# Layer two's second products: tokens or weights as the stationary side, and another table of priorities

## The chip, the cores and the metric

The kernel runs on one core of one Trainium2 chip. Times are device microseconds of one execution. An execution that is profiled also has a span, which the profiler counts from the core's first instruction to its last; the device time lies a little above it. The engines are PE (TensorE matmuls), PEld (TensorE weight loads), DVE (VectorE), ACT (ScalarE), POOL and SP, which issues nearly all transfers.

## The reference

Local attention over 3072 tokens (24 tiles of 128), then two layers of the same shape, each a product into 2048 hidden columns, a gate, and a product back to 512:

```python
x = attention(q, k, v, mem_k, mem_v)                 # 3072 x 512
h = x @ moe_w_in                                     # 512 -> 2048
x = (s * np.maximum(h, 0.0) ** 2 + b) @ moe_w_out    # 2048 -> 512
h = x @ moe2_w_in
g = h * (1.0 / (1.0 + np.exp(-1.702 * h)))
return (g @ moe2_w_out).astype(np.float32)           # 3072 x 512
```

All inputs are float32 (the weights come in a wider form, of which the kernel makes float32 words).

## The kernel before

Every product that needs float32 accuracy is made of three matmuls in the faster fp32r form: each operand is cut into a high part (a cast) and a low part (what the cast left over), and high by high, high by low and low by high are added up in PSUM.

The work on PE has three parts. First come attention for all tiles, woven together with layer one for 2048 of the tokens (lines 711 and 744, `step`). Then four stages of `wino(s)` follow, each for 1024 tokens in two blocks `bp` and `bq` of 512. `SEVEN` lists them: stage 0 is the rest of layer one (`m = 0`), stages 1 to 3 are layer two (`m = 1`). A stage does both of its large products with seven block products in place of eight, after Winograd.

In a stage, the first products (`product`, lines 1082 to 1084) make the gated hidden values G, in eight chunks `p` of 128 hidden rows by 512 tokens for each of four types. The second products then run seven times, in the order `n = 0, 4, 1, 5, 3, 6, 2`, each over eight chunks `p`; one call of `outer_product(n, p, ...)` is one chunk of one product. It takes G's high and low part (`gh`, `gl`, 128 by 512 tokens) and the weights' high and low part (`wh`, `wl`, 128 by 256 output columns), and adds to a pair of PSUM banks.

The two layers differed in how this was done. For `m = 0` the weights are stationary in two pieces of 128 output columns and 512 tokens stream past (line 1243): six matmuls of 512 columns, output with columns on the partitions. For `m = 1` the tokens are stationary in four pieces of 128 and 256 weight columns stream past (line 1237): twelve matmuls of 256 columns, output with tokens on the partitions, as the result wants it:

```python
if m:
    for t in range(4) if only is None else only:
        ...
        for x, (lt, rh) in enumerate(((gh, wh), (gh, wl), (gl, wh))):
            nc.tensor.matmul(a, lt[:, z], rh, ...)
```

What feeds these chunks is `split` (lines 1204 and 1207): ACT casts two chunks of G at once into a tile `kh`, and DVE subtracts to make `kl`. There are three pairs of such tiles (two in the ring `wj`, one in the ring `q`; the trace calls them `oj` and `oq`). ACT's cast for a pair therefore waits until PE has read the last of that pair. Weights come by SP (line 1182) into a ring of eight. For the products 3, 6 and 2, DVE first adds or subtracts types of G (line 1216). After the seven products DVE and ACT add the banks up in a tile `ys` (lines 1253, 1265, 1306), and SP stores (lines 1272, 1274). The very last product of the last stage is cut into pieces (`only`), with its own additions and stores in `last` (lines 1290 and 1295).

The order of all work is fixed when the program is built. `Plan.order` lists every operation with a due time, moves the due times by the table `SHIFTS` (operation number, how many from there on, by how much), and then picks for each engine what is due first among what is ready in its own model of times. Where the model sees PE idle at the start, it puts in filler matmuls (line 1407, `idle`).

Of the kernel before, what the change touches and what calls it, by code (L numbers as in the profile page):

```python
# [12 lines left out]
ALU = mybir.AluOpType  # L13
AX = mybir.AxisListType

P = 128
# [4 lines left out]
NT = B * S  # L21
DM = H * D
DFF = 2048
KT = DM // P
# [77 lines left out]
)  # L102
# [174 lines left out]
def attention_moe_moe(ctx: ExitStack, tc: tile.TileContext, q_t, k_w, v_w, w_in1, w_out1, s_b, w_in2, w_out2, out):  # L277
# [504 lines left out]
    def finish(m, b, k, group, lo, hi, after, need):  # L782
# [16 lines left out]
        def store(e):  # L799
            if m == 0:  # L800
                dst = y1[k, :, b * 512:b * 512 + 512]
            else:
                dst = out[(4 * b + k) * P:(4 * b + k + 1) * P, :]
            nc.sync.dma_start(out=dst, in_=T["y", m, b, k])

# [222 lines left out]
    def wino(s):  # L1028
# [189 lines left out]

        extra = ("turn", s, "a", 2)

        def outer_product(n, p, need, key, d, after, only=None):
            tag, turn = BANKS[n]
            held = ("turn", s, tag, turn)
            ending = s == len(SEVEN) - 1 and n == 2
            first = n != 5 and p == 0

            def fn(e):
                acc = psum(tag, held)
                gh, gl = [T[key + (v,)][:, p % 2] for v in "hl"]
                wh, wl = [w[:, p % 2 * 256:p % 2 * 256 + 256] for w in T["wp", s, n, p // 2]]  # L1230
                if m:
                    for t in range(4) if only is None else only:
                        z = slice(t * P, t * P + P)
                        own = ending and t == 3
                        a = psum("a", extra)[:, 0][:, :256] if own else acc[:, t // 2, t % 2 * 256:t % 2 * 256 + 256]
                        for x, (lt, rh) in enumerate(((gh, wh), (gh, wl), (gl, wh))):
                            nc.tensor.matmul(a, lt[:, z], rh, start=first and (own or t % 2 == 0) and x == 0,  # L1237
                                             stop=p == HALF - 1 and x == 2, skip_group_check=True)
                else:
                    for k in range(2):  # L1240
                        z = slice(k * P, k * P + P)
                        for x, (lt, rh) in enumerate(((wh, gh), (wh, gl), (wl, gh))):
                            nc.tensor.matmul(acc[:, k], lt[:, z], rh, start=first and x == 0,  # L1243
                                             stop=p == HALF - 1 and x == 2, skip_group_check=True)
            return op(need, {"pe": 0.36 * len(only) if only is not None else 1.44 if m else 1.36}, fn, after=o_part[n, p // 2] + [d] + after, alloc=taken(tag, held) + (taken("a", extra) if ending else []),
                      uses=[("wp", s, n, p // 2), key + ("h",), key + ("l",), held] + ([extra] if ending else []))

# [10 lines left out]
        def away(n, b, in1, need, after, lo, q, where=None):  # L1258
# [8 lines left out]
            def store(e):  # L1267
                t = (bq if q else bp) * 512
                if m:
                    r = t + b * 256  # L1270
                    dst = out[r:r + 256, 0 if lo else 256:256 if lo else 512].rearrange("(t p) d -> p t d", p=P)
                    nc.sync.dma_start(out=dst, in_=T[key].rearrange("p (t d) -> p t d", t=2))
                else:
                    nc.sync.dma_start(out=y1[(0 if lo else 2) + b, :, t:t + 512], in_=T[key])
            d = op(need, {"dve": 0.69}, fn, after=(o_end[n] if held else []) + after, alloc=[("y", key)] if where is None else [],
# [8 lines left out]
        def last(n, b, part, need, after, end):  # L1284
            held = ("turn", s) + BANKS[n]
            lo, hi = (part, part + 1) if b else (0, 2)
            z = slice(256 * lo, 256 * hi)

            def fn(e):
                nc.vector.tensor_tensor(out=spot(b)[:, z], in0=T[extra][:, 0][:, :256] if b and part else T[held][:, b][:, z], in1=spot(b)[:, z], op=ALU.add)  # L1290

            def store(e):
                r = bp * 512 + b * 256
                dst = out[r + lo * P:r + hi * P, 256:512].rearrange("(t p) d -> p t d", p=P)
                nc.sync.dma_start(out=dst, in_=spot(b)[:, z].rearrange("p (t d) -> p t d", t=hi - lo))
            d = op(need, {"dve": 0.42 if b else 0.69}, fn, after=[end] + after, uses=[tmp, extra if b and part else held])
            o = op(need, {"sp": 0.37 if b else 0.73}, store, after=[d], uses=[tmp])
            plan.soon.update((d, o))
# [12 lines left out]
        for i, n in enumerate((0, 4, 1, 5, 3, 6, 2)):  # L1311
# [3 lines left out]
            for x in range(HALF // 2):  # L1315
# [8 lines left out]
                for p in (2 * x, 2 * x + 1):  # L1324
                    if s == len(SEVEN) - 1 and n == 2 and p == HALF - 1:
                        prev = [outer_product(n, p, here + 8 * p + only[0], key, d, prev + wait, only) for only in ((0, 1), (2,), (3,))]
                    else:
                        prev = [outer_product(n, p, here + 8 * p, key, d, prev + wait)]
            o_end[n] = prev
            e = here + 66  # L1330
            for b in range(2):
# [9 lines left out]
                elif n == 6:  # L1341
                    got["u4", b] = evac(n, b, b, b, e, [got["u2", b], got["c21", b]])
                    got["c22", b] = away(None, b, b, e, [got["u4", b], got["y7", b]], False, True, 2 + b)
                elif n == 2:
                    if s == len(SEVEN) - 1:
                        for part in range(b + 1):
                            last(n, b, part, e, [got["u4", b], got["c22", b]], o_end[n][b + part])
                    else:
                        away(n, b, b, e, [got["u4", b], got["c22", b]], False, False, b)
# [61 lines left out]

_OUTS = [((NT, DM), "float32")]

# [52 lines left out]
```

## Time and profile before

| | us |
|---|---|
| median of 3 runs | 1062.87 (1062.79 to 1063.54) |
| profiled execution, device time | 1063.68 |
| its span | 1061.9 |
| PE busy | 1049.8 (99%) |
| DVE busy | 758.4 (71%) |
| ACT busy | 602.4 (57%) |
| transfers | 265.67 MB, 250 GB/s over the span |

The profiled execution took 0.81 us longer than the median of the runs. A row of the page's fifth part reads: line, engine, operation, what is written from what, shape, count, then busy time and mean duration of one. Matmuls are pipelined, so the duration of one matmul record is longer than its pace; the pace is read from the starts of matmuls that follow each other, or from the length of a long run of them in the chain of work.

### The profile page before, as it was taken

Reading aid. Unit: us, or ns where it says so; the run is one execution under the profiler, and the core shown is the slowest. Engines: PE = TensorE matmul, PEld = TensorE weight load, DVE = VectorE, ACT = ScalarE, POOL = GpSimd, SP = SyncE. Lnnn points to the kernel's source line nnn. Section 1 sums busy time; section 2 is a strip of 40 time slices with the busy share of each in tenths; the row PEclk is TensorE's granted clock in tenths of the full one; section 3 lists DMA queues with packets and bytes.
Section 4 is the critical chain, followed back from the end, with each engine's and each line's share of the span. In section 5 each row is a group of like instructions: output and inputs, shape, how many; then the busy total and the mean of one; then the engine's idle time right before and its main releaser. Section 6 shows DMA issues by size and latency. Waiting matters only on the chain.

```text
span 1061.9 us, 21584 instructions
## 1 busy us (share of the span) xinstructions
PE 1049.8 (99%) x8573; PEld 904.0 (85%) x8573; DVE 758.4 (71%) x1145; ACT 602.4 (57%) x932; POOL 0.7 (0%) x6
## 2 busy tenths in 40 slices
PE   7999999999999999999999999999999999999998
PEld 5787888888888888888888888999888999888998
DVE  6996996889898668888999446985224984222954
ACT  6776765546666557888744556542455542454432
POOL 0000000000000000000000000000000000000000
PEclk9999999999999999999999999999999999999999
DMA  9679854758899855997978998776656676666662
GB/s 348 229 248 342 291 187 178 263 187 255 294 353 359 304 208 204 322 341 264 343 259 285 303 341 285 242 241 205 209 183 201 204 240 207 201 195 196 209 201 80
DMA packets 151556, 265.67 MB, mean 250 GB/s; under 512 B 14240, under 2 KB 65440, under 8 KB 151456
## 3 DMA queue, kind: packets, MB, share of 16 engines
q1 hardware_dynamic: 151168, 263.77, 74.0%
q8 instruction: 68, 1.11, 0.4%
q10 hardware_dynamic: 288, 0.52, 0.1%
q14 instruction: 32, 0.26, 0.1%
HBM read 190.84 MB, written 73.40 MB: 249 GB/s over the span
## 4 chain that ended last, share of the span: by engine, by line
PE 93%; DVE 1%; ACT 1%; DMA 1%; issue 0%; DVEq 0%; SPq 0%; ACTq 0%
PE ph L711 15%; PE pc L1237 9%; PE accA L744 8%; PE accB L744 8%; PE pb L1237 7%; PE pd L1237 7%; PE pc L1243 3%; PE ph L1082 3%; PE pd L1082 3%; PE ph L1084 3%; PE ph L1083 3%; PE pd L1083 3%; PE pd L1084 3%; PE pb L1082 2%; PE pc L1082 2%; PE pc L1083 2%
## 5 line engine op out<-in xcount | busy, mean ns | idle before, releaser
L1207 DVE TENSOR_TENSOR oj<-G,oj 128x1024 fp32r<-128x1024 f32 x72 | 87.6, 1220 | 49.5 <-ACT oj L1204 49.3
L1204 ACT CAST oj<-G 128x1024 fp32r<-128x1024 f32 x72 | 75.3, 1051 | 80.9 <-PE pd L1237 30.1
L717 ACT ACTIVATE r<-ph 128x512 f32<-128x512 f32 (+1 forms) x66 | 38.6, 584 | 65.0 <-PE ph L711 38.5
L1204 ACT CAST oq<-G 128x1024 fp32r<-128x1024 f32 x40 | 42.1, 1052 | 50.7 <-PE pc L1237 18.7
L1207 DVE TENSOR_TENSOR oq<-G,oq 128x1024 fp32r<-128x1024 f32 x40 | 48.8, 1221 | 28.8 <-ACT oq L1204 28.8
L1094 ACT ACTIVATE G<-ys 128x512 f32<-128x512 f32 x64 | 40.4, 632 | 40.4 <-DVE ys L1136 40.1
L1237 PE MATMUL pc<-wih,oj 128*128 128x256 f32 x328 | 61.6, 283 | 0.0
L732 ACT CAST gh<-r 128x512 fp32r<-128x512 f32 (+1 forms) x66 | 40.1, 607 | 31.0 <-PE accB L744 21.2
L1216 DVE TENSOR_TENSOR G<-G 128x1024 f32<-128x1024 f32 x48 | 57.1, 1218 | 0.1
L736 DVE TENSOR_TENSOR gl<-r,gh 128x512 fp32r<-128x512 f32 (+1 forms) x66 | 44.2, 670 | 17.0 <-ACT gh L732 13.8
L1237 PE MATMUL pd<-wih,oj 128*128 128x256 f32 x288 | 54.1, 283 | 0.0
L1237 PEld LDWEIGHTS pc<-wih,oj 128*128 128x128 f32 x328 | 52.3, 192 | 0.0
L435 ACT ACTIVATE u<-st 128x512 f32<-128x512 f32 x64 | 42.9, 671 | 11.6 <-DMA st<-w_in 7.5
L1237 PE MATMUL pb<-wih,oj 128*128 128x256 f32 x248 | 47.2, 283 | 0.0
L1237 PE MATMUL pc<-wil,oj 128*128 128x256 f32 x164 | 46.4, 283 | 0.0
L1237 PEld LDWEIGHTS pd<-wih,oj 128*128 128x128 f32 x288 | 45.9, 192 | 0.0
L1237 PE MATMUL pc<-wih,oq 128*128 128x256 f32 x232 | 44.7, 283 | 0.0
L447 DVE SCALAR_TENSOR_TENSOR u<-u,st 128x512 uint32<-128x512 uint32 x64 | 43.5, 686 | 1.2
L443 ACT ACTIVATE st<-st 128x512 uint32<-128x512 uint32 x64 | 42.9, 672 | 1.0 <-DMA st<-w_in 1.0
L453 DVE SCALAR_TENSOR_TENSOR u<-st,u 128x512 uint32<-128x512 uint32 x64 | 43.2, 684 | 0.4
L744 PE MATMUL accA<-gh,woh 128*128 128x512 f32 (+1 forms) x132 | 42.0, 393 | 0.0
L724 ACT ACTIVATE r<-r 128x512 f32<-128x512 f32 (+1 forms) x66 | 40.8, 619 | 1.6
(253 smaller groups left out, 2997.6 us busy)
## 6 DMA issues: line engine op xcount, KB each, us to landing
wih<-wodh SPq DMA_DIRECT2D x112, 256.0 KB, 3.2
wil<-wodl SPq DMA_DIRECT2D x112, 256.0 KB, 3.8
wih<-wch SPq DMA_DIRECT2D x96, 256.0 KB, 3.7
wil<-wcl SPq DMA_DIRECT2D x96, 256.0 KB, 4.0
st<-w_in SPq DMA_DIRECT2D x32, 512.0 KB, 5.8
st<-w_out SPq DMA_DIRECT2D x32, 512.0 KB, 5.9
k<-k_w SPq DMA_DIRECT2D x24, 512.0 KB, 6.1
v<-v_w SPq DMA_DIRECT2D x24, 512.0 KB, 6.1
```

What stands on the lines that cost most here:

```text
L447: nc.vector.scalar_tensor_tensor(out=u, in0=u, scalar=3, in1=T["st", i][:, :, 0], op0=ALU.logical_shift_left, op1=ALU.bitwise_or)
L453: nc.vector.scalar_tensor_tensor(out=u, in0=T["st", i][:, :, 1], scalar=0x80000000, in1=u, op0=ALU.bitwise_and, op1=ALU.bitwise_or)
L711: nc.tensor.matmul(T["ph", i], T[win][x][:, k * P:(k + 1) * P], T["x", m, b][y][:, k, r], start=seen_["hid"] == 1, stop=seen_["hid"] == 3 ...
L736: nc.vector.tensor_tensor(out=gl, in0=T["r", i], in1=gh.bitcast(F32), op=ALU.subtract)
L744: nc.tensor.matmul(T["acc", group, k // 2][:, k % 2][:, r], T[wout][x][:, k * P:k * P + P], T["g", i][y], start=fresh and (x, y) == (0, 0) ...
L1082: nc.tensor.matmul(ph, wh, xh, start=first and i == 0, stop=False, skip_group_check=True)
L1083: nc.tensor.matmul(ph, wh, xl, start=False, stop=False, skip_group_check=True)
L1084: nc.tensor.matmul(ph, wl, xh, start=False, stop=i == 1, skip_group_check=True)
L1204: nc.scalar.copy(out=T[kh], in_=g_of(ty, z))
L1207: nc.vector.tensor_tensor(out=T[kl], in0=g_of(ty, z), in1=T[kh].bitcast(F32), op=ALU.subtract)
L1216: o_raw[out, x] = [op(need, {"dve": 1.22}, lambda e: nc.vector.tensor_tensor(out=g_of(out, z), in0=g_of(a, z), in1=g_of(b, z), op=o), afte ...
L1237: nc.tensor.matmul(a, lt[:, z], rh, start=first and (own or t % 2 == 0) and x == 0, stop=p == HALF - 1 and x == 2, skip_group_check=True)
```

## The change

Layer two's second products take the form that layer one's have: weights stationary, 512 tokens streaming. `outer_product` loses its branch for `m = 1`; the kernel's output is an array of four times 128 output columns by 3072 tokens, and the host turns it round after the run. `away` and `last` add and store in that layout: a store now writes 128 rows of 512 tokens, where it wrote 128 tokens in two pieces of 256 columns. The last chunk of the last product is cut in two pieces (a bank each) where it was cut in three, and no longer borrows a PSUM pair for one of them.

```diff
-                if m:
-                    for t in range(4) if only is None else only:
-                        z = slice(t * P, t * P + P)
-                        own = ending and t == 3
-                        a = psum("a", extra)[:, 0][:, :256] if own else acc[:, t // 2, t % 2 * 256:t % 2 * 256 + 256]
-                        for x, (lt, rh) in enumerate(((gh, wh), (gh, wl), (gl, wh))):
-                            nc.tensor.matmul(a, lt[:, z], rh, start=first and (own or t % 2 == 0) and x == 0,
-                                             stop=p == HALF - 1 and x == 2, skip_group_check=True)
-                else:
-                    for k in range(2):
-                        z = slice(k * P, k * P + P)
-                        for x, (lt, rh) in enumerate(((wh, gh), (wh, gl), (wl, gh))):
-                            nc.tensor.matmul(acc[:, k], lt[:, z], rh, start=first and x == 0,
-                                             stop=p == HALF - 1 and x == 2, skip_group_check=True)
+                for k in only:
+                    z = slice(k * P, k * P + P)
+                    for x, (lt, rh) in enumerate(((wh, gh), (wh, gl), (wl, gh))):
+                        nc.tensor.matmul(acc[:, k], lt[:, z], rh, start=first and x == 0,
+                                         stop=p == HALF - 1 and x == 2, skip_group_check=True)
...
-                if m:
-                    r = t + b * 256
-                    dst = out[r:r + 256, 0 if lo else 256:256 if lo else 512].rearrange("(t p) d -> p t d", p=P)
-                    nc.sync.dma_start(out=dst, in_=T[key].rearrange("p (t d) -> p t d", t=2))
-                else:
-                    nc.sync.dma_start(out=y1[(0 if lo else 2) + b, :, t:t + 512], in_=T[key])
+                nc.sync.dma_start(out=(out if m else y1)[(0 if lo else 2) + b, :, t:t + 512], in_=T[key])
...
-    (2775, 16, 1.52), (1101, 1, 10.64),
+    (2775, 16, 1.52), (1101, 1, 10.64), (128, 4, -10.11), (128, 1, -0.03), (30, 1, -0.33), (1, 1, 8.83),
...
-                        prev = [outer_product(n, p, here + 8 * p + only[0], key, d, prev + wait, only) for only in ((0, 1), (2,), (3,))]
+                        prev = [outer_product(n, p, here + 8 * p + only[0], key, d, prev + wait, only) for only in ((0,), (1,))]
...
-_OUTS = [((NT, DM), "float32")]
+_OUTS = [((KT, P, NT), "float32")]
...
-    return r.results[0]["out_0"]
+    return np.ascontiguousarray(r.results[0]["out_0"].reshape(DM, NT).T)
```

The table `SHIFTS` gets 83 more entries, from operation 1 on to the end, so the order changes in all parts of the program; eight older entries that ran past the last operation are only cut to its number. Counted over the whole program, the instructions of DVE, ACT, SP and POOL stay the same in kind and shape but for a few copies and gate steps that move between ACT and DVE, the layouts of layer two's stores and the last additions. On PE, 2016 matmuls of 256 columns become 1008 of 512, fillers go from 19 to 17, and all else is equal in number.

The last chunk of the last product, on PE before (`pb` and `pc` are PSUM banks, `oq` G's two parts, `wih` and `wil` the weights' two parts; the token pieces stand in the order 2, 0, 1, 3):

```order
L1237 MATMUL pc_11697<-wih_11600,oq_11754 128x256
L1237 MATMUL pc_11697<-wil_11601,oq_11754 128x256
L1237 MATMUL pc_11697<-wih_11600,oq_11755 128x256
L1237 MATMUL pc_11696<-wih_11600,oq_11754 128x256
L1237 MATMUL pc_11696<-wil_11601,oq_11754 128x256
L1237 MATMUL pc_11696<-wih_11600,oq_11755 128x256
L1237 MATMUL pc_11696<-wih_11600,oq_11754 128x256
L1237 MATMUL pc_11696<-wil_11601,oq_11754 128x256
L1237 MATMUL pc_11696<-wih_11600,oq_11755 128x256
L1237 MATMUL pb_11707<-wih_11600,oq_11754 128x256
L1237 MATMUL pb_11707<-wil_11601,oq_11754 128x256
L1237 MATMUL pb_11707<-wih_11600,oq_11755 128x256
```

The same chunk, on PE of the changed kernel:

```order
L1242 MATMUL pc_10740<-oq_10772,wih_10686 128x512
L1242 MATMUL pc_10740<-oq_10773,wih_10686 128x512
L1242 MATMUL pc_10740<-oq_10772,wil_10687 128x512
L1242 MATMUL pc_10739<-oq_10772,wih_10686 128x512
L1242 MATMUL pc_10739<-oq_10773,wih_10686 128x512
L1242 MATMUL pc_10739<-oq_10772,wil_10687 128x512
```

Twelve matmuls became six, G's part moved from the stationary to the streaming side, and both pieces go to the product's own two banks, the second bank first.

DVE just after the start, before, where the second token tile's scores are reduced (`top`) and lessened (`qe`), and words of the weights are put together (`u`; the file's line numbers move by some 15 in the changed kernel):

```order
L538 TENSOR_REDUCE top_273<-sc_227 128x8
L453 SCALAR_TENSOR_TENSOR u_214<-st_154,u_214 128x512
L541 TENSOR_TENSOR qe_150<-sc_227,top_273 128x2x4x64
L439 TENSOR_SCALAR u_271<-u_271 128x512
L413 TENSOR_TENSOR wil_320<-u_214,wih_319 128x512
```

The same place on DVE of the changed kernel:

```order
L553 TENSOR_REDUCE top_273<-sc_227 128x8
L454 TENSOR_SCALAR u_271<-u_271 128x512
L556 TENSOR_TENSOR qe_150<-sc_227,top_273 128x2x4x64
L462 SCALAR_TENSOR_TENSOR u_271<-u_271,st_170 128x512
L468 SCALAR_TENSOR_TENSOR u_214<-st_154,u_214 128x512
```

The subtraction into `qe` no longer stands behind the step that ends the first weight word (line 453, now 468), but behind a shorter one (line 439, now 454).

DVE a little later, before, around the normalising products of the third and fourth tile (line 587, which wait for the sums `den`):

```order
L587 TENSOR_TENSOR px<-o,den 128x2x4x64
L564 TENSOR_REDUCE den<-qe 128x8
L567 TENSOR_SCALAR den<-den 128x8
L568 RECIPROCAL den<-den 128x8
L439 TENSOR_SCALAR u<-u 128x512
L587 TENSOR_TENSOR px<-o,den 128x2x4x64
```

The same place on DVE of the changed kernel:

```order
L579 TENSOR_REDUCE den<-qe 128x8
L582 TENSOR_SCALAR den<-den 128x8
L583 RECIPROCAL den<-den 128x8
L454 TENSOR_SCALAR u<-u 128x512
L602 TENSOR_TENSOR px<-o,den 128x2x4x64
L462 SCALAR_TENSOR_TENSOR u<-u,st 128x512
L602 TENSOR_TENSOR px<-o,den 128x2x4x64
```

The fourth tile's sum has moved ahead of the third tile's product, so that only one weight step stands between the two products.

## Rows read from the trace of the kernel before

**Rows 1.** The page, parts 1 and 2: busy us, and the granted TensorE clock.

```profile
PE 1049.8 (99%) x8573; PEld 904.0 (85%) x8573; DVE 758.4 (71%) x1145; ACT 602.4 (57%) x932; POOL 0.7 (0%) x6
...
PEclk9999999999999999999999999999999999999999
```

**Rows 2.** Busy time by stretch, PE alone: stretch, length, PE busy, clock, DMA share, GB/s.

```profile
33.00:300.00 267.00, 266.40 (x2856) 1.00 0.75 251
300.00:600.00 300.00, 299.89 (x2170) 1.00 0.85 296
600.00:1058.00 458.00, 457.98 (x2962) 1.00 0.67 216
```

**Rows 3.** PE's waits, first and last of nine: us in total, times, longest.

```profile
PE o L582 <- issue: 1.6, 2, 1.2
...
PE o L582 <- ACT px L313: 0.2, 1, 0.2
```

**Rows 4.** The chain that ended last, in order of time: start, us, engine, tile, line, count.

```profile
520.33 10.88 PE pc L1243 x48
...
988.87 11.52 PE pc L1237 x96
1000.39 11.52 PE pd L1237 x96
```

**Rows 5.** Busy time by stretch, second products: PE, PEld, DVE, ACT, POOL, clock, DMA, GB/s.

```profile
506.70:587.00 80.30, 80.30 (x356) 66.50 (x355) 75.58 (x96) 44.81 (x57) 0.00 (x0) 1.00 0.86 296
...
822.70:899.00 76.30, 76.30 (x637) 76.30 (x637) 62.33 (x70) 30.95 (x34) 0.00 (x0) 1.00 0.70 222
```

**Rows 6.** Timeline, casts of `split` on ACT: layer one's stage, then layer two's.

```profile
539.18 1.06 ACT L1204 CAST oj<-G 128x1024 fp32r<-128x1024 f32 x1 [1.66 <-PE pd L1243]
541.90 1.06 ACT L1204 CAST oj<-G 128x1024 fp32r<-128x1024 f32 x1 [1.66 <-PE pd L1243]
...
1011.83 1.05 ACT L1204 CAST oj<-G 128x1024 fp32r<-128x1024 f32 x1 [1.83 <-PE pd L1237]
1014.71 1.05 ACT L1204 CAST oq<-G 128x1024 fp32r<-128x1024 f32 x1 [1.83 <-PE pc L1237]
```

**Rows 7.** Timeline, the subtraction of `split` on DVE in layer two's last stage.

```profile
1021.54 1.23 DVE L1207 TENSOR_TENSOR oj<-G,oj 128x1024 fp32r<-128x1024 f32 x1 [1.66 <-ACT oj L1204]
```

**Rows 8.** PE's groups in the first 33 us: busy us, mean ns.

```profile
L1407 PE MATMUL idle<-cold 128*128 128x512 f32 x19 | 6.3, 427 | 0.0
```

**Rows 9.** Timeline of PE near the start, two places.

```profile
12.99 0.66 PE L554 MATMUL pp<-ident,qe 128*128 128x128 f32 x4 [0.26 <-ACT qe L546]
...
30.69 0.65 PE L596 MATMUL xx<-ident,px 128*128 128x128 f32 x4 [0.57 <-DVE px L587]
```

**Rows 10.** Timeline of DVE near the start, at those places.

```profile
11.00 0.68 DVE L453 SCALAR_TENSOR_TENSOR u<-st,u 128x512 uint32<-128x512 uint32 x1
11.60 0.68 DVE L541 TENSOR_TENSOR qe<-sc,top 128x512 f32<-128x512 f32 x1
...
28.62 0.68 DVE L564 TENSOR_REDUCE den<-qe 128x8 f32<-128x512 f32 x1
...
29.95 0.68 DVE L587 TENSOR_TENSOR px<-o,den 128x512 f32<-128x512 f32 x1
31.15 0.68 DVE L447 SCALAR_TENSOR_TENSOR u<-u,st 128x512 uint32<-128x512 uint32 x1
```

**Rows 11.** Timeline of PE and DVE at the end.

```profile
1057.66 0.69 DVE L1290 TENSOR_TENSOR ys<-pc,ys 128x512 f32<-128x512 f32 x1 [0.29 <-PE pc L1237]
1057.70 0.28 PE L1237 MATMUL pb<-wih,oq 128*128 128x256 f32 x1
1058.27 0.41 DVE L1290 TENSOR_TENSOR ys<-pb,ys 128x256 f32<-128x256 f32 x1
```

**Rows 12.** Line 1295, the last three stores (two of 128 KB, one of 256 KB).

```profile
DMA to landing us min/median/max: 1.7/2.1/2.2
```

**Rows 13.** Line 1272, layer two's other stores (256 KB each).

```profile
DMA to landing us min/median/max: 2.2/3.1/6.5
```

More of the change, by code (lines that the diff above doesn't have):

```diff
@@ L799, in store @@
         def store(e):
-            if m == 0:
-                dst = y1[k, :, b * 512:b * 512 + 512]
-            else:
-                dst = out[(4 * b + k) * P:(4 * b + k + 1) * P, :]
-            nc.sync.dma_start(out=dst, in_=T["y", m, b, k])
+            nc.sync.dma_start(out=y1[k, :, b * 512:b * 512 + 512], in_=T["y", m, b, k])
         acc = ("acc", group, k // 2)
@@ L1217, in sums, with outer_product @@
                 out=g_of(out, z), in0=g_of(a, z), in1=g_of(b, z), op=o), after=after + o_raw[a, x] + o_raw[b, x])]
-        extra = ("turn", s, "a", 2)
-        def outer_product(n, p, need, key, d, after, only=None):
+        def outer_product(n, p, need, key, d, after, only=(0, 1)):
             tag, turn = BANKS[n]
             held = ("turn", s, tag, turn)
-            ending = s == len(SEVEN) - 1 and n == 2
             first = n != 5 and p == 0
@@ L1230, in fn @@
                 wh, wl = [w[:, p % 2 * 256:p % 2 * 256 + 256] for w in T["wp", s, n, p // 2]]
-                if m:
-                    for t in range(4) if only is None else only:
-                        z = slice(t * P, t * P + P)
-                        own = ending and t == 3
-                        a = psum("a", extra)[:, 0][:, :256] if own else acc[:, t // 2, t % 2 * 256:t % 2 * 256 + 256]
-                        for x, (lt, rh) in enumerate(((gh, wh), (gh, wl), (gl, wh))):
-                            nc.tensor.matmul(a, lt[:, z], rh, start=first and (own or t % 2 == 0) and x == 0,
-                                             stop=p == HALF - 1 and x == 2, skip_group_check=True)
-                else:
-                    for k in range(2):
-                        z = slice(k * P, k * P + P)
-                        for x, (lt, rh) in enumerate(((wh, gh), (wh, gl), (wl, gh))):
-                            nc.tensor.matmul(acc[:, k], lt[:, z], rh, start=first and x == 0,
-                                             stop=p == HALF - 1 and x == 2, skip_group_check=True)
-            return op(need, {"pe": 0.36 * len(only) if only is not None else 1.44 if m else 1.36}, fn, after=o_part[n, p // 2] + [d] + after, alloc=taken(tag, held) + (taken("a", extra) if ending else []),
-                      uses=[("wp", s, n, p // 2), key + ("h",), key + ("l",), held] + ([extra] if ending else []))
+                for k in only:
[3 more added lines that the diff above has]
+                                         stop=p == HALF - 1 and x == 2, skip_group_check=True)
+            return op(need, {"pe": 0.68 * len(only)}, fn, after=o_part[n, p // 2] + [d] + after, alloc=taken(tag, held),
+                      uses=[("wp", s, n, p // 2), key + ("h",), key + ("l",), held])
         def evac(n, b, out, in1, need, after):
@@ L1268, in store @@
                 t = (bq if q else bp) * 512
-                if m:
-                    r = t + b * 256
-                    dst = out[r:r + 256, 0 if lo else 256:256 if lo else 512].rearrange("(t p) d -> p t d", p=P)
-                    nc.sync.dma_start(out=dst, in_=T[key].rearrange("p (t d) -> p t d", t=2))
-                else:
-                    nc.sync.dma_start(out=y1[(0 if lo else 2) + b, :, t:t + 512], in_=T[key])
+                nc.sync.dma_start(out=(out if m else y1)[(0 if lo else 2) + b, :, t:t + 512], in_=T[key])
             d = op(need, {"dve": 0.69}, fn, after=(o_end[n] if held else []) + after, alloc=[("y", key)] if where is None else [],
@@ L1285, in last @@
             held = ("turn", s) + BANKS[n]
-            lo, hi = (part, part + 1) if b else (0, 2)
-            z = slice(256 * lo, 256 * hi)
+            z = slice(256 * part, 256 * part + 256) if b else ALL
             def fn(e):
-                nc.vector.tensor_tensor(out=spot(b)[:, z], in0=T[extra][:, 0][:, :256] if b and part else T[held][:, b][:, z], in1=spot(b)[:, z], op=ALU.add)
+                nc.vector.tensor_tensor(out=spot(b)[:, z], in0=T[held][:, b][:, z], in1=spot(b)[:, z], op=ALU.add)
             def store(e):
[L1293 to L1296, printed above, removed]
+                nc.sync.dma_start(out=out[2 + b, :, bp * 512 + z.start:bp * 512 + z.stop], in_=spot(b)[:, z])
+            d = op(need, {"dve": 0.42 if b else 0.69}, fn, after=[end] + after, uses=[tmp, held])
             o = op(need, {"sp": 0.37 if b else 0.73}, store, after=[d], uses=[tmp])
@@ L1346, in wino @@
                         for part in range(b + 1):
-                            last(n, b, part, e, [got["u4", b], got["c22", b]], o_end[n][b + part])
+                            last(n, b, part, e, [got["u4", b], got["c22", b]], o_end[n][b])
                     else:
```

31 rows, old and new, of the table SHIFTS are left out of this document.

## The prediction

> **What bounds the kernel now.** I read the page first: PE is busy 99% of the span at full granted clock (2.4 GHz), the other engines 71% and less [rows 1]. Then busy time by stretch: from 33 us to 1058 us PE lacks 0.60, 0.11 and 0.02 us, so nearly all that it does not use lies in the first 33 us and in the last 4 [rows 2]. PE's list of waits says the same: nine kinds, from 1.6 down to 0.2 us [rows 3]. So almost everywhere the end is set by how much PE has to issue. A step that makes PE's work shorter shortens the run by as much, as long as those who feed PE keep up; a step that makes another engine's work shorter does nothing.
>
> A matmul's duration is no measure of that work, since matmuls overlap. What counts is the pace. The chain of waits shows long unbroken runs of both forms of the second products: 48 matmuls of 512 columns took 10.88 us in layer one, 96 of 256 columns took 11.52 us in layer two, for the same amount of arithmetic [rows 4]. That is 226.7 ns and 120.0 ns each. Two matmuls of 256 cost 240.0 ns where one of 512 costs 226.7: each merged pair saves 13.3 ns. It looks like a fixed price per matmul beside its columns.
>
> **The main step.** Layer two has three stages of seven second products, and each product is a run as in [rows 4]: 21 runs, 21 x 96 = 2016 matmuls, which become 21 x 48 = 1008. Each run goes from 11.52 to 10.88 us, if 512 columns cost in layer two what they cost in layer one: 21 x 0.64 = 13.44 us less. All of it lies on the path that sets the end, because PE is full in these stretches [rows 5]. The form is not new to the kernel: same tiles, same ring, same weights' layout, only the layer differs. So I take the row of layer one as it is.
>
> **Does the feed keep up?** The same casts, subtractions and transfers must now be done in 10.88 in place of 11.52 us. Layer one's stretch shows the answer at just that pace: there DVE is busy 75.58 of 80.30 us (94%) and the transfers 86%, and PE is full for all 80.30 us. In layer two DVE is busy 62.33 of 76.30 us; shrunk by 10.88/11.52 the stretch is 72.1 us, so DVE would be 86% busy, and the transfers go from 70% to some 74%, both below layer one [rows 5]. Closer: ACT's casts for `split` wait for PE, which still reads the tiles, for 1.66 us of every 2.72 in layer one and 1.83 of every 2.88 in layer two [rows 6]. The feeder waits for PE, not PE for the feeder; DVE in turn waits 1.66 us for ACT [rows 7]. I cost this at nothing, and the 1.6 us of slack per cast is the cover.
>
> **The start.** The fillers on PE took 6.3 us of the first 33 [rows 8], and waits lie between them; here PE follows attention's chain through DVE and ACT. Two moves of the new order bear on that. The second tile's subtraction loses the 0.68 us step ahead of it (rows at 11.00 and 11.60) and stands behind a shorter one that ran later anyway; PE's transposes at 12.99 waited for just that tile's exponential, so they may come 0.6 us earlier [rows 9, 10]. And the fourth tile's normalising product, which began at 29.95, stood behind the sum at 28.62 and what follows it; with the sum done earlier only a weight step of 0.68 is left between it and the third tile's product, after which that sum began: 0.6 to 0.7 us earlier, and PE's transposes at 30.69 waited for it. Against it stands that ACT now makes a weight step before the first tile's copy, some 0.6 us later for that tile, which costs perhaps 0.4 us if it shows. The term lies between -1.3 and +0.4; I take -0.6, one of the two moves, because after 33 us PE is full and can pass a gain on only if the weights are ready earlier too.
>
> **The end.** Before, the last matmul starts at 1057.70 and ends 0.28 later, at 1057.98; DVE's last addition ends at 1058.27 + 0.41 = 1058.68, so 0.70 us after PE [rows 11]. The changed order has the bank with the two half additions first and the 512-wide addition last: some 0.04 us to start and 0.69 us, 0.73 after PE. The last store is then 256 KB in place of 128. The three stores of the end landed in 1.7 to 2.2 us, one of 256 KB among them [rows 12]; others of 256 KB took 3.1 in the middle [rows 13]. The bounds of this term are -0.4 and +1.1 us; I take +0.1, since at the end nothing else is in the queue, as for the three.
>
> **The rest.** All else of the new order I cost at nothing: PE's instructions in these parts are the same in kind and number, PE has hardly a wait there to lose [rows 2], and the changes between attention's small matmuls and the large ones are nearly as many (104 before, 105 now). What hides the reordering is the slack of DVE and ACT; if it fails, rival two prices it.
>
> **The sum.** Against the profiled execution's 1063.68 us: -13.44 - 0.6 + 0.1 gives 1049.7. The median of the runs lies 0.81 us lower, at 1062.87, and so the forecast for the median is 1048.9 us, 1.3% faster.
>
> **The rivals.**
> *One, slower: the ring of split tiles becomes the bound.* Three pairs of tiles serve two chunks each. A freed pair is needed again after two other pairs have been used up: 2 x 2.88 = 5.76 us before, 5.44 now. In that time ACT's 1.05 and DVE's 1.22 us must pass, with whatever DVE has queued ahead. If a turn takes x us more than 5.44, PE waits x for each of 3 x 28 = 84 splits. At x = 0.16 us the gain is gone, from 0.185 us the run is slower by over 0.2%; at 0.25 us it would end at 1048.9 + 21 = 1070. For it: DVE's additions and the next stage's inputs are queued between the subtractions. Against it: layer one ran at that pace with DVE fuller and without a wait of PE [rows 5, 6]. 4 in 100, half of them at or beyond no change.
>
> *Two: the new order makes PE wait in attention and layer one.* The ten remaining pairs of tiles enter PE four times each. If half of these 40 entries waited the 0.4 us that lies between the two waits of [rows 9], that is 8 us: 1057. For it: the order moves in all parts, and PE takes its instructions strictly as they stand. Against it: before, waits of that kind came to 0.6 us over 267 us [rows 2]. 8 in 100.
>
> *Three: columns cost, not instructions.* If the pace of 120.0 ns for 256 columns were what this layer's data cost, 512 columns would cost 240 and nothing would be saved: 1062.4 with the start and the end alone. Against it: layer one's 226.7 is measured on the same kind of operands [rows 4]. 2 in 100. Beside it stands a rule of the Trainium skill (TensorE: Matmul & The Clock Gate, section Back-to-back issue gap): a lone warm matmul of N columns follows the next after N/2.4 + 2.5 ns, so the price per instruction would be 2.5 ns. By that rule the pace would be 109.2 and 215.8 ns, merging would save 1008 x 2.5 = 2.5 us, and the run would end near 1060. The trace does not agree at either size (120.0 and 226.7 ns); the page says itself that weight loads between the matmuls make the real spacing another.
>
> **Chances and range.** The forecast's own case has 84 in 100: with the bounds of start and end it spans 1062.87 - 13.44 - 1.3 - 0.4 = 1047.7 to 1062.87 - 13.44 + 0.4 + 1.1 = 1050.9. The rivals have 4, 8 and 2; 2 are left for gains that I do not see. The range reaches a little into rival two, for a microsecond of new waits: 1047.2 to 1052.0. A measurement of this kernel tells 0.2% (2.1 us) from no change. Faster by more: 95 in 100; within it 2.5 (most of rival three, a part of one and two); slower 2.5 (half of rival one, and what of rival two is far worse).
>
> **What would show it.** In the changed profile the chain has runs of 48 matmuls in 10.88 us in layer two, the second products' matmuls are 1008 with line 1242 alone, each of the three stretches is 4.5 us shorter, and PE still lacks under 1 us between 33 us and its end. ACT's casts there wait some 1.66 us for PE. Rival one would show as waits of PE for DVE's subtraction in these stretches; rival two as waits of PE before 500 us; rival three as 11.5 us for 48 matmuls. At the start the first 33 us would have less filler and PE's first large matmuls would stand up to a microsecond earlier. The prediction is wrong if PE's own work shrinks by 13.4 us and the span does not follow: then something other than PE set the pace, unseen in the list of waits.

## The result and the profile after

| | before | after |
|---|---|---|
| median, us (range, runs) | 1062.83 (1061.82 to 1063.54, 4) | 1048.80 (1048.40 to 1049.46, 4) |
| profiled execution: span, us | 1061.9 | 1046.4 |
| PE busy, us | 1049.8 | 1034.9 |

The ratio is 0.9869, 95% interval 0.9852 to 0.9886: 14.0 us less, against the 13.9 that the sum gave. Parts 1 and 2 of the changed kernel's page answer to [rows 1]: PE is still busy 99% at the full clock, and it is PE's busy time that shrank, by 14.9 us, while DVE's and ACT's moved by less than 2 us.

```profile
PE 1034.9 (99%) x7563; PEld 850.8 (81%) x7563; DVE 756.7 (72%) x1144; ACT 603.8 (58%) x933; POOL 0.7 (0%) x6
...
PEclk9999999999999999999999999999999999999999
```

The chain that ended last (start, us, engine, tile, line, count) answers to [rows 4]. Here are three of layer two's products, one in each stage:

```profile
671.56 10.88 PE pc L1242 x48
...
824.41 10.88 PE pc L1242 x48
...
988.20 10.88 PE pd L1242 x48
```

Layer two now has layer one's pace to the last digit. From the start of layer one's last second product to PE's end it was 481.89 us before (576.09 to 1057.98) and is 468.13 us now (574.47 to 1042.60): 13.76 us less, where 13.44 were forecast for the 21 products.

PE's busy time by stretch answers to [rows 2] (stretch, length, PE busy, clock, DMA share, GB/s). PE ends at 1042.60, so the last row lacks nothing before that point:

```profile
33.00:300.00 267.00, 266.40 (x2934) 1.00 0.75 251
300.00:600.00 300.00, 299.92 (x2072) 1.00 0.85 295
600.00:1044.00 444.00, 442.60 (x1946) 1.00 0.69 222
```

ACT's casts for `split` answer to [rows 6], and a stretch of second products in layer two's middle stage to [rows 5]. The cast waits 1.67 us of each 2.72 for PE, as forecast; DVE is busy 61.31 of 73.44 us (83%; 86% was worked out) and the transfers 74%.

```profile
1004.33 1.05 ACT L1215 CAST oj<-G 128x1024 fp32r<-128x1024 f32 x1 [1.67 <-PE pc L1242]
1007.05 1.05 ACT L1215 CAST oj<-G 128x1024 fp32r<-128x1024 f32 x1 [1.67 <-PE pc L1242]
```

```profile
816.09:889.53 73.44, 73.44 (x326) 60.83 (x324) 61.31 (x68) 32.34 (x38) 0.00 (x0) 1.00 0.74 233
```

The result itself leaves three things open: whether the gain came from the form or from the table, why two matmuls of 256 columns cost more than one of 512, and how near the feed was to its limit.

### The profile page after: what moved, and what is told of

It reads as the page before. It is cut to its first block, busy times and chain, and to the rows that moved or that the text cites. A ratio compares the mean times of both kernels' runs of the same rounds, so it can differ in the third digit from the quotient of the medians.

```text
span 1046.4 us, 19645 instructions
## 1 busy us (share of the span) xinstructions
PE 1034.9 (99%) x7563; PEld 850.8 (81%) x7563; DVE 756.7 (72%) x1144; ACT 603.8 (58%) x933; POOL 0.7 (0%) x6
## 4 chain that ended last, share of the span: by engine, by line
PE 80%; DVE 4%; DMA 3%; issue 0%; ACT 0%; SPq 0%; DVEq 0%
PE pc L1242 12%; PE ph L726 9%; PE pb L1242 8%; PE pd L1242 8%; PE accA L759 5%; PE accB L759 5%; PE ph L1093 3%; PE pd L1093 3%; PE ph L1095 3%; PE pd L1095 3%; PE ph L1094 3%; PE pd L1094 3%; PE pb L1094 2%; PE pb L1093 2%; PE pc L1093 2%; PE pc L1094 2%
## 5 line engine op out<-in xcount | busy, mean ns | idle before, releaser
L1242 PE MATMUL pc<-oj,wih 128*128 128x512 f32 x224 | 69.0, 389 | 0.0
L1242 PE MATMUL pd<-oj,wih 128*128 128x512 f32 x192 | 59.1, 389 | 0.0
L747 ACT CAST gh<-r 128x512 fp32r<-128x512 f32 (+1 forms) x66 | 39.9, 605 | 25.2 <-PE accB L759 15.1
L1242 PE MATMUL pb<-oj,wih 128*128 128x512 f32 x160 | 49.3, 389 | 0.0
L1242 PE MATMUL pc<-oq,wih 128*128 128x512 f32 x160 | 49.3, 389 | 0.0
L1242 PEld LDWEIGHTS pc<-oj,wih 128*128 128x128 f32 x224 | 42.1, 188 | 8.7
L1242 PE MATMUL pc<-oj,wil 128*128 128x512 f32 x112 | 43.6, 389 | 0.0
L1242 PEld LDWEIGHTS pd<-oj,wih 128*128 128x128 f32 x192 | 36.0, 188 | 7.4
```

## The experiments

### The table alone and the form alone

The first kernel is the kernel before with the changed kernel's table (the edit below), the second the changed kernel with the table of before (the edit turned round):

```diff
 SHIFTS = (
...
-    (2775, 16, 1.52), (1101, 1, 10.64),
+    (2775, 16, 1.52), (1101, 1, 10.64), (128, 4, -10.11), (128, 1, -0.03), (30, 1, -0.33), (1, 1, 8.83),
...
 )
```

> The kernel before with nothing changed but the table of priorities, which is that of the changed kernel. Theory (PE-bound; the form of the products gives 13.4 us, the table only what the start gains, 1.6 us by the two traces): 1061.2 us, runs of 96 matmuls still in 11.52 us, PE at its first 512-wide matmul 1 to 2 us earlier than the 39.3 us of before. Rival (the table also takes waits out of layer two): below 1059 us, and layer two's stages shorter than before.

> The changed kernel with the table of priorities of the kernel before. Theory: 1050.4 us, that is 1048.8 and the 1.6 us of the start; runs of 48 matmuls in 10.88 us, PE without a wait in layer two. Rival (the shorter products need the new order to be fed): over 1052 us, with waits of PE for DVE's subtraction or for transfers in the three stretches of second products.

| | median, us | ratio to before (95%) |
|---|---|---|
| table alone | 1061.37 | 0.9987 (0.9978 to 0.9996) |
| form alone | 1049.44 | 0.9876 (0.9862 to 0.9889) |
| both | 1048.80 | 0.9869 (0.9852 to 0.9886) |

By the ratios the form gives 13.2 us, the table 1.4 (0.4 to 2.3); on the occasion of the first two the kernel before took 1062.52 us. In the chain of the kernel with the table alone layer two's runs are as in the kernel before:

```profile
997.90 11.52 PE pd L1252 x96
1009.42 11.52 PE pc L1252 x96
```

With the form alone PE's list of waits (us in total, times, longest; the first of a longer list) has none in layer two. Line 744 is layer one's, line 368 the first filler's, the others attention's; lines 1227 (second products) and 1078 to 1080 (first products) do not stand in it at all:

```profile
PE warm L368 <- DVE cold L348: 1.5, 1, 1.5
PE pp L554 <- ACT qe L546: 1.3, 2, 0.7
PE sc L521 <- DMA k<-k_w: 1.1, 1, 1.1
PE xx L596 <- DVE px L587: 1.0, 3, 0.6
PE accB L744 <- ACT ys L313: 1.0, 1, 1.0
```

So the form did not need the new order. Since 0.6 us between "form alone" and "both" is too little for runs taken on different occasions, both went to one chip together.

> The changed kernel once more, on one chip with the next. If the table is worth what it gave the kernel before (1.4 us, interval 0.4 to 2.3): 1.4 us below the next kernel. If the table is worth nothing with the new form: within 0.5 us of it.

> The changed kernel with the table of priorities of the kernel before, on one chip with the kernel above. Table worth 1.4 us: about 1050.2 us to the other's 1048.8. Table worth nothing with the new form: within 0.5 us of the other.

The changed kernel took 1047.62 us (1046.87 to 1048.28), the one with the old table 1049.73 (1048.77 to 1050.12). The ranges do not touch: the table is worth some 2 us with the new form too. On this occasion the kernel before took 1062.69 us, so the changed kernel is 15.1 us below it (ratio 0.9856, 0.9840 to 0.9873) where the result had 14.0. Where the table's gain lies is shown by a mark that all kernels have, the first second product of layer one's stage in the chain. With the old table it starts at 506.73 (before), 506.57 and 506.39 us (the two runs of the form alone); with the new one at 504.01 to 505.91 in nine profiles (the changed kernel twice, the table alone, and the kernels below), 505.0 in the mean: 1.6 us earlier. PE's first 512-wide matmul, near 38 us, shows only a part of that, and no clear one: 39.31, 37.80 and 37.91 with the old table, 37.26 to 38.33 with the new. How the 1.6 us are shared out before that mark is not settled: from the first 512-wide matmul to the mark it takes 467.42, 468.77 and 468.48 us with the old table and 466.20 to 468.20 with the new, 1.1 us less in the mean, but the ranges overlap. Of PE's waits in between, only one belongs to the table: some 0.6 us on ACT's `qe` near 51 us, which all three profiles with the old table have and none of the nine with the new. A wait of layer one's line 744 (759 in the changed kernel) on ACT's `ys`, of 0.2 to 1.3 us, stands in some profiles of either table.

The second run of the form alone lost 0.6 us more behind the mark, and there its list of waits does have a line of layer two, in the first products of the last stage, at 903.67 us:

```profile
PE pb L1078 <- ACT ys L1126: 0.4, 1, 0.4
```

No profile with the form alone has a wait in the second products.

### Is it the number of matmuls, or the side that streams?

The first of these kernels cuts each 512-wide matmul of layer two in two (`w = 256` in the edit), with weights still stationary; the second cuts it in four (`w = 128`), the third in 384 and 128. Order, layout and stores stay those of the changed kernel.

```diff
                 for k in only:
                     z = slice(k * P, k * P + P)
-                    for x, (lt, rh) in enumerate(((wh, gh), (wh, gl), (wl, gh))):
-                        nc.tensor.matmul(acc[:, k], lt[:, z], rh, ...)
+                    for c in range(0, 512, w):
+                        for x, (lt, rh) in enumerate(((wh, gh), (wh, gl), (wl, gh))):
+                            nc.tensor.matmul(acc[:, k][:, c:c + w], lt[:, z], rh[:, c:c + w], ...)
```

> The changed kernel with each of layer two's 512-wide second-product matmuls cut into two of 256 tokens, weights still stationary: 2016 matmuls again, same order of all work, same layout, same stores. Theory (a fixed price of 13.3 ns per matmul beside its columns): 1048.8 + 13.4 = 1062.2 us, 96 matmuls in 11.52 us. Rival (the price hung on the side, tokens stationary and weights streaming): 1049 us, 96 matmuls in 10.88 us.

> The same cut into four of 128 tokens: 4032 matmuls. 256 columns more cost 226.7 - 120.0 = 106.7 ns, so 128 columns are 53.3 ns of streaming. Theory (fixed price): 66.7 ns each, 192 in 12.8 us, 1048.8 + 40.3 = 1089 us. Rival (a matmul can't follow the last one faster than its weights load; the 120 ns of a 256-wide matmul were already that floor): 120 ns each, 192 in 23 us, 1048.8 + 255 = 1304 us. Between the two the floor lies between 67 and 120 ns.

> The changed kernel with each 512-wide second-product matmul of layer two cut into one of 384 and one of 128 tokens, weights stationary. By the runs of 48 and 96 and the quarters: 512 columns 226.7 ns, 256 columns 120.0 ns, 128 columns 111.7 ns. Theory (13.3 ns per matmul beside 53.3 ns for each 128 columns, and never under 111.7 ns): 173.3 + 111.7 ns, 96 matmuls in 13.68 us, 1048.8 + 21 x 2.80 = 1107.6 us. Rival (cost goes with columns above the floor, 226.7 x 384/512 = 170.0 ns): 13.52 us, 1104.2 us.

The halves took 1062.25 us (ratio to before 0.9990, 0.9981 to 1.0000), 13.45 more than the changed kernel, with the chain's runs back at the old length. The nearest partner is the kernel with the table alone, which has the same table and the other form, on the same occasion: 1061.37 us. So the side that is stationary, the layout and the stores have no price beyond the 0.9 us between these two; the count has.

```profile
830.44 11.52 PE pc L1244 x96
841.96 11.52 PE pd L1244 x96
```

The quarters took 1269.38 us, 220.6 more than the changed kernel, and here the theory of a fixed price fell: it had 1089. The chain gives the pace, 21.44 / 192 = 111.7 ns, where the theory had 66.7 and the rival 120.0:

```profile
1134.92 21.44 PE pc L1244 x192
1156.36 21.44 PE pd L1244 x192
```

So 128 columns cost hardly less than 256. The timeline of the weight loads has three in every 0.33 us, one for each matmul, at the matmuls' own pace.

```profile
1150.77 0.30 PEld L1244 LDWEIGHTS pc<-oj,wih 128*128 128x128 f32 x2
1151.00 0.19 PEld L1244 LDWEIGHTS pc<-oj,wil 128*128 128x128 f32 x1
1151.11 0.30 PEld L1244 LDWEIGHTS pc<-oj,wih 128*128 128x128 f32 x2
```

That fits a floor set by the loads, since every matmul brings its own load of 128 by 128. But any floor for such a pair would show the two at one pace, and PE's loads are busy all the time at 256 columns already [rows 5]; so that the loads are the cause is argued, not shown, as no run changed their size. Nor is the floor the rate at which PE takes a load and a matmul as such: attention's pairs, each a load of 64 by 32 and 64 columns on a part of the array, come 64 in 0.85 us in the same trace.

```profile
8.37 0.85 PE L536 MATMUL sc<-k,qe 64*32 64x64 f32 x64 [1.05 <-DMA k<-k_w]
```

The Trainium skill (TensorE: Matmul & The Clock Gate, section LDWEIGHTS (loading the stationary operand)) gives a load of P columns as P/1.2 ns, which makes an estimate of 106.7 ns for these 128. The measured floor of a load and its matmul is 111.7, near it; a single load's record lasts 190 ns in this trace and overlaps the next, so it gives no price of a load by itself.

The uneven cut took 1109.96 us in a single run, against 1107.6 for the theory and 1104.2 for the rival. Its chain has 96 matmuls in 13.81 us:

```profile
847.03 13.81 PE pc L1243 x96
860.84 13.81 PE pd L1243 x96
```

A pair of 384 and 128 thus costs 287.7 ns (285.0 by the theory, 281.7 by the rival). Both fall short. If the 128 take their 111.7 ns, the 384 take 176.0, 16.0 beside their columns, where the theory had 13.3. With a single run, this is the only test of the price between the widths: the 53.3 ns for 128 columns are half the step from 256 to 512, so that the 13.3 at these two widths is one number and no proof of a fixed price. Together, for one load and one matmul in this form:

| columns | ns each | beside 53.3 ns for 128 columns |
|---|---|---|
| 512 | 226.7 | 13.3 |
| 256 | 120.0 | 13.3 |
| 128 | 111.7 | 58.3 |

At 256 columns the kernel before was 8.3 ns above the 111.7 ns of 128 columns. What the 13.3 ns are stays open.

### How near is the feed to its limit?

Three kernels make the feed of layer two's second products worse: ACT's cast done twice, two pairs of tiles in place of three, DVE's subtraction done twice.

```diff
                 nc.scalar.copy(out=T[kh], in_=g_of(ty, z))
+                if m:
+                    nc.scalar.copy(out=T[kh], in_=g_of(ty, z))
```

```diff
-            tag = "wj" if rung[0] % 3 else "q"
+            tag = "wj" if m or rung[0] % 3 else "q"
```

```diff
                 nc.vector.tensor_tensor(out=T[kl], in0=g_of(ty, z), in1=T[kh].bitcast(F32), op=ALU.subtract)
+                if m:
+                    nc.vector.tensor_tensor(out=T[kl], in0=g_of(ty, z), in1=T[kh].bitcast(F32), op=ALU.subtract)
```

> The changed kernel with ACT's cast of every split in layer two done twice (84 more casts of 1.05 us, 88 us more work on ACT), order of all else the same. Theory (the feeder waits for PE: 1.67 us of each 2.72 us, and a freed pair has 5.44 us): a turn takes 1.05 us more, 2 x 1.05 + 1.22 = 3.3 of 5.44 us; 1049 to 1050 us, PE without a wait. Rival (the feed is at its limit at the new pace): up to 84 x 1.05 us later, over 1055 us, PE waiting for DVE's subtraction.

The cast done twice took 1051.06 us, ratio 0.9894 (0.9877 to 0.9910), 1 us above the upper end of the theory and far under the rival: 2.3 us more than the changed kernel's 1048.80, and 3.4 more than the 1047.62 of its second occasion. In the stretch of second products it cost nothing, as the same stretch of the changed kernel above shows (73.44 us): PE is full in both, with 26 us more of ACT here.

```profile
818.14:891.58 73.44, 73.44 (x325) 60.83 (x324) 61.52 (x68) 58.37 (x63) 0.00 (x0) 1.00 0.72 233
```

What was lost lies elsewhere. Against the first profile of the changed kernel, PE ends 2.8 us later. The first products of the first layer-two stage took 69.52 us (585.96 to 655.48) in place of 68.47 (585.18 to 653.65), with a wait of PE for ACT of 0.6 us at 638.92: the first doubled casts there stand ahead of ACT's copies for PE. Some 0.8 us more went in the first products of the last stage, with a wait of 0.4 us at 930.49. The changed kernel has neither wait, so "PE without a wait" missed them. Another 0.8 us was lost before layer two's work begins, which this edit cannot reach; it lies within what profiles of one table differ by.

```profile
PE pd L1093 <- ACT pd L1137: 0.6, 1, 0.6
...
PE ph L1093 <- ACT pb L1137: 0.4, 1, 0.4
```

> The changed kernel with two pairs of split tiles in layer two in place of three (the ring of one pair is not used there). A freed pair is needed again after 2.72 us, and cast and subtraction take 2.27 us and two hand-overs. Theory (the third pair is what covers the feed): the turn is missed wherever DVE has a 1.22 us sum ahead, which is in three of seven products: 36 splits by some 0.3 to 1.2 us, 1060 to 1095 us, PE waiting for DVE's subtraction in the products 3, 6 and 2. Rival (the cover is larger than that): 1049 to 1051 us.

Two pairs took 1056.54 us, ratio 0.9952 (0.9936 to 0.9967): 7.7 us more than the changed kernel's 1048.80 (8.9 more than its second occasion), between the two expectations and under the theory's lower end of 11 us. PE waits for DVE's subtraction behind a sum, as named, but not where it was named: DVE makes the sums for the products 3, 6 and 2 ahead, and PE's waits stand in the products 4, 1 and 5, with one of 0.2 us in the last. Line 1242 sat idle 22 times for 13.0 us in matmuls and loads together, and of these the matmuls' own part, as far as the list has it, is

```profile
PE pd L1242 <- DVE oj L1218: 2.5, 3, 1.1
...
PE pc L1242 <- DVE oj L1218: 0.8, 3, 0.4
```

Two of the longest, at the start of the third product (1) of two stages:

```profile
687.78 0.50 PE L1242 MATMUL pd<-oj,wih 128*128 128x512 f32 x1 [1.08 <-DVE oj L1218]
...
998.75 0.50 PE L1242 MATMUL pd<-oj,wih 128*128 128x512 f32 x1 [1.07 <-DVE oj L1218]
```

With the ring cut down the planner also ordered the work anew, so this is the price of the ring with an order made for it.

> The changed kernel with DVE's subtraction of every split in layer two done twice (28 more per stage at a pace of 1.14 us, 32 us). DVE is busy 61.3 us of a stretch of 73.5 us, so 93 us of work no longer fit. Theory (PE sets the pace only while DVE fits): DVE becomes the bound there, each of three stretches grows by some 15 to 20 us, 1094 to 1109 us, PE waiting for the subtraction. Rival (there is slack elsewhere that takes it up): under 1060 us.

The subtraction done twice took 1097.57 us in a single run, 48.8 more than the changed kernel and in the range of the theory. In a stretch of layer two's middle stage PE is no longer full (74.30 of 90 us), and DVE is at 95% (from and to, length, then PE, PEld and DVE busy):

```profile
840.00:930.00 90.00, 74.30 (x306) 55.90 (x305) 85.78 (x87) 29.00 (x34) 0.00 (x0) 1.00 0.54 175
```

The list of waits names the releaser that rival one was to show by; the six lines of this kind, of which three stand here, come to 35.6 us:

```profile
PE pd L1244 <- DVE oj L1220: 11.1, 10, 2.8
PE pc L1244 <- DVE oj L1220: 8.7, 9, 1.6
PE pc L1244 <- DVE oq L1220: 7.1, 7, 2.2
```

## Why the prediction was right, point by point

**The bound.** PE set the pace: every change of PE's work came out in the time (13.2 us by the form alone, 13.45 back by the halves), and 88 us more work on ACT cost 2 to 3.5.

**The main step, 13.44 us.** Right in size (13.2 us by the form alone, with an interval of 11.8 to 14.7; 10.88 us a run in the chain) and in where it lies. The reason given with it, a fixed price per matmul, fits 256 and 512 columns and is wrong as a rule: 384 columns came out at some 16 ns beside their columns, and at 128 a floor of 111.7 ns has taken over. The forecast did not rest on it, since both of its widths had their own rows [rows 4]; had the change gone from 128 to 256 columns, the same reasoning would have seen 13.3 ns in each merged pair where there were 2 x 111.7 - 120.0 = 103 to gain. That the total met the sum within 0.1 us is in part luck: the table gave more than was forecast and the form a little less, and on the second occasion the same kernel came out 1.2 us lower.

**The feed at nothing.** Right: no wait of PE in layer two, and ACT's slack of 1.67 us per cast was real, as the doubled cast showed. The price of rival one, x us for each of 84 splits, was not tested: no run made a turn longer by a known x. The doubled subtraction lost 0.58 us a split and the two pairs 0.09. (The 0.185 us from which that rival would have been slower counts against the main step alone; against the whole forecast it is 0.19.)

**The start, -0.6 us.** Right for the table's part near the start in the mean (0.5 us at the first 512-wide matmul, over three and nine profiles), but that is no more than the profiles of one table differ among themselves. Of the two moves, the second did what was said of it: the fourth tile's product on DVE stands 1.19 us after the third's where it was 1.93 [rows 10], 0.7 us earlier by that. The first shows less: PE's transposes of the second tile stand at 12.88 us with no wait, 0.1 us before [rows 9] though that tile's keys landed 0.5 us later; in the changed kernel's second profile they stand at 12.91 and wait 0.28 us for ACT. And the term that stood against it did show: the first tile's second product of attention on PE (line 582, now 597) moved from 11.22 to 12.09 us, 0.5 us of it by the keys, and PE's waits for ACT's `px` grew from 0.2 us [rows 3] to 1.0. Before, then in the changed kernel:

```profile
11.22 0.85 PE L582 MATMUL o<-v,px 64*32 64x64 f32 x64 [0.44 <-DMA v<-v_w]
...
28.02 0.69 DVE L587 TENSOR_TENSOR px<-o,den 128x512 f32<-128x512 f32 x1 [1.60 <-PE o L582]
```

```profile
PE o L597 <- ACT px L328: 1.0, 3, 0.5
```

```profile
12.09 0.86 PE L597 MATMUL o<-v,px 64*32 64x64 f32 x64 [0.32 <-ACT px L328]
...
12.88 0.66 PE L569 MATMUL pp<-ident,qe 128*128 128x128 f32 x4
...
26.77 0.69 DVE L602 TENSOR_TENSOR px<-o,den 128x512 f32<-128x512 f32 x1
...
27.96 0.69 DVE L602 TENSOR_TENSOR px<-o,den 128x512 f32<-128x512 f32 x1
```

The profiled execution of before was a poor witness here. Its first 512-wide matmul stood at 39.31 us; the same table gave 37.80 and 37.91 in the two other profiles. By the mark near 505 us that lag was down to 0.2 to 0.3 us, so it is not why the two spans differ by 15.5 us and the medians by 14.0: the profiled execution of before took 0.85 us more than its median and that of the changed kernel 0.40 less.

**The rest at nothing.** This term was too small, on the good side: the table as a whole gave 1.4 to 2.1 us where start and rest had 0.6, and 1.6 us of that lie before the mark near 505 us. About 1 us of it falls between 38 and 505 us in the mean, which the overlap of the ranges leaves unproven. PE's busy time from 33 to 300 us cannot show it, for it is 266.40 us in both profiles.

**The end, +0.1 us.** The last addition ended 0.73 us after PE, as worked out (1043.33 and 1042.60), the stores landed in 1.7 to 2.0 us where they took 1.7 to 2.2 [rows 12], and the span ended 3.8 us after PE where it was 3.9: -0.1 in place of +0.1.

```profile
1041.96 1.37 DVE L1283 TENSOR_TENSOR ys<-pc,ys 128x256 f32<-128x256 f32 x3 [4.67 <-PE pc L1242]
```

**The rivals.** Rival one did not occur, and the doubled subtraction shows what it would have looked like. Rival two did not occur as a loss; the new order brought waits of up to 0.5 us in attention and layer one and took others away, and the list's sum went from 8.1 to 7.3 us, while the other profiles lie at 7.5 and 7.7 with the old table and at 5.9 to 8.4 with the new one and the feed as it was. Rival three is refuted by the changed kernel itself (48 matmuls in 10.88 us), and with it, for this kernel, the 2.5 ns per matmul of the Trainium skill's rule (TensorE: Matmul & The Clock Gate, section Back-to-back issue gap): a merged pair gave 13.3 ns, whichever side was stationary.

## What to carry to other kernels

Where PE is full, read the pace of each width from long runs in the chain and count matmuls: the wide form is worth (2 x the pace of the narrow one - the pace of the wide one) per merged pair, whichever operand is stationary, if the result's layout can be had for nothing; here the host turns it round, which is no part of the time measured. A second form of the same step in the same kernel is the best witness there is, since it shows the pace and the feed at that pace at once. Terms below a microsecond need more than one profile: profiles with one and the same table differed by 1 to 1.5 us within the first 40.

## What was not expected of the hardware

A matmul of 128 columns with its own weight load paced at 111.7 ns, and one of 256 at 120.0: halving the streamed columns below 256 saved 7%. And two pairs of split tiles, with 2.72 us for a turn that needs 2.27 us of ACT and DVE, cost only 8 to 9 us over 84 turns.
